# Two products with B sooner, turnings one scan step sooner, and 512 columns a matmul in ten products

## The chip, the cores and the metric

The kernel runs on one core of one Trainium2 chip. The metric is the device time of one launch in microseconds (us); the comparison is with the kernel before, on the same chip. Engines are called by the profile's names: PE (matmuls), PEld (its weight loads), DVE (vector), ACT (scalar), POOL and SP (which here mostly issue DMAs).

## The reference, cut to what is computed

All inputs are bf16; S = 2048 positions, D = 1024 channels, P = 1024 states.

```
x  = A_x
g  = sigmoid(sum(x * gate_w))                       # one gate per position
# branch A: a diagonal complex state space
Bu = x @ B_bar^T                                    # B_bar = (Lam_bar - 1)/Lam * (B_re + i B_im)
h[t] = Lam_bar * h[t-1] + Bu[t]                     # for t = 0..2047
a  = 2 * Re(h @ C^T) + x * Dskip
# branch B: a 4-tap filter, a product, a long convolution over 2048 positions
kv = shift_filter(k, shift_k) * v
b  = x * (conv(kv, ssm_k) + kv * ssm_D)
out = g * a + (1 - g) * b
```

## The kernel before

The first half (to about 212 us) does branch B: the long convolution as products with tables of cosines and sines, with its result `cv_scr` left in DRAM. The second half does most of branch A. The change lies almost wholly there.

**Tiling.** Positions come in `NTB` = 4 time blocks `tb` of 512, states in `NG` = 4 groups `g` of 256 (two tiles `j` of 128). In a time block the positions are split in odd and even ones, 256 each (`HB`): the scan runs over even positions only, with the squared factor, and odd ones follow from it. So there are 16 *scan steps* `j` = 0..15, one for each (`tb`, `g`), all on DVE.

**B products.** `Bu(i)` makes the input of one scan step; here `B8` is the product number 8. The list `order` says which (`tb`, `g`) a number stands for: the scan steps 4..15 use the numbers 2, 3, 8, 9, 4, 5, 10, 11, 12, 13, 14, 15. A product has two tiles, each made by `Bu_plain` (numbers 4, 5 and 8 to 15) or `Bu_tile` (the others). `Bu_plain` makes an *odd* and an *even* accumulator in PSUM, each with 16 matmuls of 256 columns, and ACT copies each to the tile U.

**Accumulators.** All products and rows draw their PSUM accumulators from one pool of four (`ps2`), in rotation: each one needs the accumulator drawn four before it to have been evicted by ACT.

**Turnings.** The products of `Bu_plain` have to be turned before their scan: `turn_U` (generators `turns_U[i]`) has ACT write lambda times the odd inputs to a buffer Q, one half of it at each of two calls, and then issues on POOL two DMAs (`gather`) that add Q to U, the second after the first has landed, as both add to the same place. There are two Q buffers: a turning waits for the second gather of the turning two before. (`turn_C`, which turns the matrices C, is another thing, and ended by step 4.)

**Rows.** `Cy_row(k)`, here `Ck`, is the product with C of 128 positions: 32 matmuls of 512 columns on PE into one accumulator, an eviction by ACT (`scale_a`, to `ga`), then `combine(k)`: a gather on POOL that adds the other branch, and on SP the write of the output; behind it on SP the loads of row k+3 (`loads`), and then on ACT `scale_b` of row k+2, which waits for that row's load (two ACTIVATEs, `pbb` and `gd`) and has a gather on POOL of its own. The last four rows are made together at the end of the kernel, from four accumulators (called F0 to F3 here), group after group of states.

**Order.** Engines run what is issued to them in order of program (`put` ties each engine's instructions to a chain). The string list `plan` gives, for each step j, the products and rows that follow the DVE work of that step; the first half of a turning is issued ahead of them (`step(turn)`), the second half and its gathers behind them (`run(turn)`).

Of the kernel before, what the change touches and what calls it, by code (L numbers as in the profile page):

```python
# [10 lines left out]
ACT = mybir.ActivationFunctionType  # L11
# [9 lines left out]
def kernel(  # L21
# [35 lines left out]
    ND = D // 128  # L57
# [3 lines left out]
    NTB = S // TB  # L61
    HB = TB // 2
# [23 lines left out]
    def ps2(shape, name):  # L86
        return psum.tile(shape, F32, name=name, tag="ps")
# [4 lines left out]
    def put(eng, f, *a, **kw):  # L92
        with tc.issue_after(prev[eng]) if eng in prev else nullcontext():
            i = f(*a, **kw)  # L94
        prev[eng] = getattr(i, "ins", i)

    def mm(o, l, r, first, last):
        put("pe", nc.tensor.matmul, o, lhsT=l, rhs=r, start=first, stop=last)
# [18 lines left out]
    def act(o, i, **kw):  # L117
        put("act", nc.scalar.activation, out=o, in_=i, **kw)
# [94 lines left out]
    BT = [bt_pool.tile([128, 2, ND, 256], BF16, name=f"BT{g}") for g in range(NG)]  # L213
# [5 lines left out]
    def load_xT(tb, halves=(0, 1), held=False):  # L219
        if 0 in halves:  # L220
            xTs[tb] = (xt_pool if tb in (1, 2) else xt_first).tile([128, ND, TB], BF16, name="xT", tag="xT")
        for h in halves:
            if held:
                hold(xTs[tb][:, 0, h * HB:h * HB + 1])
            load_t(xTs[tb][:, :, h * HB:(h + 1) * HB], xf[tb * TB + h:(tb + 1) * TB:2, :])
# [13 lines left out]
    def flat(ap):  # L239
        return ap.rearrange("p a b -> p (a b)")  # L240
# [412 lines left out]
    def gate(tb):  # L653
        psg = ps2([128, 2, 512], "p")[:, 0, 0:4]
        for tl in range(4):
            for dt_ in range(ND):
                mm(psg[:, tl:tl + 1], xTs[tb][:, dt_, tl * 128:(tl + 1) * 128], gwb[:, dt_:dt_ + 1],
                   dt_ == 0, dt_ == ND - 1)
        gates_of(slice(tb * 4, tb * 4 + 4), psg)
# [13 lines left out]
    ends = consts.tile([128, 2, NG, 2, 2], BF16, name="ends")  # L673
# [12 lines left out]
    def Bu(i):  # L686
        tb, g = order[i]
        if i in (10, 11):
            if i == 10:
                s5p["u2"] = xt_pool.tile([128, 2, 2 * (4 * HB + 4)], BF16, name="U2", tag="xT")  # L690
            U = s5p["u2"][:, i - 10]
        else:
            shape = [128, 2 * (4 * HB + 4)]
            if i in (6, 7, 8, 15):
                U = u4(shape, BF16, "U")
            else:
                home = uu[0 if i in (0, 1, 13, 14) else 1] if i < 6 or i in (13, 14) else s5p["uu"]
                U = home.tile(shape, BF16, name="U")
        if i in (4, 5) or i >= 8:
            V_, O_ = U[:, 0:4 * HB], U[:, 4 * HB:]  # L700
            V_ = V_.rearrange("p (c j t) -> p c j t", c=2, j=2)
            O_ = O_.rearrange("p (c j t) -> p c j t", c=2, j=2)
            Us[tb, g] = V_, O_[:, :, :, 2:]
            turns_U[i] = turn_U(g, V_, O_)
            return [Bu_plain(tb, g, V_, O_, j) for j in range(2)]
        U = U[:, 0:8 * HB].rearrange("p (a c j t) -> p a c j t", a=2, c=2, j=2)
        Us[tb, g] = U[:, 0], U[:, 1]
        return [Bu_tile(tb, g, U, j, (i, j) == (2, 1)) for j in range(2)]
# [25 lines left out]
    turns_U = {}  # L734

    def Bu_plain(tb, g, V_, O_, j):
        xT = xTs[tb]
        if j == 0:
            act(O_[:, :, :, 1], ends[:, 1 - tb % 2, g], func=ACT.Copy)
        for a, o in ((1, O_[:, :, j, 2:]), (0, V_[:, :, j])):  # L740
            ps = ps2([128, 2, HB], ("even", "odd")[a])
            for c in range(2):
                for dt_ in range(ND):
                    mm(ps[:, c], BT[g][:, c, dt_, j * 128:(j + 1) * 128], xT[:, dt_, a * HB:(a + 1) * HB],
                       dt_ == 0, dt_ == ND - 1)
            act(o, ps, func=ACT.Copy)
            if a == 1 and j == 1 and tb < NTB - 1:
                act(ends[:, tb % 2, g], O_[:, :, :, HB + 1], func=ACT.Copy)
        yield

    def turn_U(g, V_, O_):
# [73 lines left out]
    def loads(t_):  # L825
        if t_ < NT - 4:
            pbb = s5p["io"].tile([128, D], BF16, name="pbb", bufs=3)
            xr = s5p["io"].tile([128, D], BF16, name="xr", bufs=3)
        else:
            pbb, xr = bt_row(0, t_ - NT + 4), bt_row(1, t_ - NT + 4)  # L830
        move(pbb.rearrange("p (c d) -> p c d", d=128), cv_scr[:, :, t_ % 4, t_ // 4].rearrange("c p d -> p c d"))
        move(xr, rows_of(xf, t_))
        ios[t_] = pbb, xr

    def scale_b(t_):

        pbb = ios[t_][0]
        act(pbb, pbb, func=ACT.Identity, scale=omg[:, t_:t_ + 1])
        if t_ < NT - 4:
            gd = s5p["io"].tile([128, D], BF16, name="gd", bufs=1)  # L840
        else:
            gd = bt_row(3, t_ - NT + 4)
        act(gd, rows_, func=ACT.Identity, scale=gcols[:, t_:t_ + 1])
        gather(pbb, gd)
# [52 lines left out]
    def step(gen):  # L897
        next(gen, None)

    def run(gen):  # L900
        for _ in gen:
            pass
# [5 lines left out]
    none = iter(())  # L908
# [139 lines left out]
    c = NC - 1  # L1048
# [103 lines left out]


    NS = NTB * NG
    plan = ["B8", "B9 B10", "B11", "B12 C0", "C1", "C2", "C3", "B13", "C4 B14", "C5", "B15 C6", "C7", "C8", "C9", "C10", "C11"]
    rows = dict(scaled=0)

    def between(j):
# [5 lines left out]
    def prepare():  # L1164
        scale_b(rows["scaled"])
        rows["scaled"] += 1
# [3 lines left out]
    def advance(j):  # L1170
        step(scans[j])
        if j + 1 < NS:
            step(scans[j + 1])
        run(scans[j])
# [12 lines left out]
    for j in range(NS):  # L1187
        if 10 <= j < 14:
            loads(j + 2)
        advance(j)  # L1190
        for t in turning[2 * j:2 * j + 2]:
            run(t)
        on_act += [lambda t=t: step(t) for t in turning[2 * j + 2:2 * j + 4] for _ in range(2)]
        turn = turns_U[{3: 8, 4: 9, 5: 4, 6: 5}.get(j, j + 3)] if 2 < j < 13 else none
        step(turn)
        for unit in plan[j].split():
            (Bu_next if unit[0] == "B" else Cy_row)(int(unit[1:]))
        run(turn)
        if j < 3:
            prepare()  # L1200
        if 11 <= j < 15:
            scale_b(j + 1)
        if j == 0:
            load_xT(3)
            loads(2)
        if j == 8:
            gate(3)

    tb = NTB - 1
    t0 = tb * 4  # L1210
    pss = []
    for tl in range(4):
        ps = ps2([128, 2, 512], "psy")
# [42 lines left out]
```

## Time and profile before

| | |
|---|---|
| median of 3 runs | 414.16 us (413.93 to 414.62) |
| the profiled execution | 414.18 us |
| its span, first to last instruction | 412.4 us |
| busy: PE / DVE / ACT / POOL | 392.5 / 381.1 / 279.6 / 65.4 us |
| mean granted TensorE clock | 0.992 |
| PE, DVE, ACT busy in 300 to 320 us | 14.16 / 19.42 / 14.38 us, clock 0.83 |
| gathers of turnings (U<-Q) | 20, 256 KB each, 4.3 us to landing (median) |

The span is read from the instructions' records; the execution's own time is 1.8 us longer. Busy times are shares of one span and say by themselves nothing of what an engine waits for: the waits and the order of time do that. Nearly all instructions go through helper functions, so they have one line (L94), and groups are told apart by the names of the tiles, as in `psy<-CT,hb` (a row), `odd<-xT,BT` (a product with B) or `U<-Q` (a turning's gather).

### The profile page before, as it was taken

To read this page: it belongs to the slowest core of one execution; us is meant where nothing else is said; L and a number is where in the kernel's file an instruction comes from. 1 tells how busy PE (TensorE), PEld (TensorE's weight loads), DVE (VectorE), ACT (ScalarE), POOL (GpSimd) and SP (SyncE) were. 2 spreads that over 40 slices of the span, in tenths; PEclk is the share of its full clock that TensorE was granted. 3 is DMA by queue.
4 is the path that set the end of the run, shared out by engine and by line. 5 is a ranking of instruction groups with operands and counts; after the bars stand their busy time and mean duration, and the time that the engine had idled before them with its cause. 6 is when DMAs were issued, how large, how long until landed. Compare 5 with 4: busy or idle time off the path is not lost. (4 is left out here: it accounts for less than half of the span.)

```text
span 412.4 us, 7364 instructions
## 1 busy us (share of the span) xinstructions
PE 392.5 (95%) x2853; PEld 246.5 (60%) x2853; DVE 381.1 (92%) x618; ACT 279.6 (68%) x420; POOL 65.4 (16%) x88
## 2 busy tenths in 40 slices
PE   8999899999999999999989999999939999999895
PEld 5456366474755666576968888644716674444342
DVE  8799999999999999998999999999899997698954
ACT  4897986969698896565655699647585475675301
POOL 3011030302011020200000000022324123343300
PEclk9999999999999999999999999999979999999999
DMA  7879994979679391596977991149895777999902
GB/s 154 154 161 223 186 264 82 219 170 216 117 118 212 66 239 31 126 133 112 194 154 165 202 197 27 27 97 196 163 198 104 151 145 159 214 233 239 195 27 103
DMA packets 128453, 63.68 MB, mean 154 GB/s; under 512 B 106265, under 2 KB 113185, under 8 KB 128418
## 3 DMA queue, kind: packets, MB, share of 16 engines
q1 hardware_dynamic: 117664, 42.22, 47.5%
q0 software_dynamic: 10672, 20.98, 29.5%
q8 instruction: 22, 0.36, 0.4%
q14 instruction: 13, 0.11, 0.1%
q10 hardware_dynamic: 82, 0.02, 0.0%
HBM read 12.86 MB, written 8.39 MB: 52 GB/s over the span
## 5 line engine op out<-in xcount | busy, mean ns | idle before, releaser
L94 PEld LDWEIGHTS <-BT 128*128 128x128 bf16 x1024 | 99.7, 98 | 13.1 <-issue 0.2
L94 PE MATMUL psy<-CT,hb 128*128 128x512 bf16 x256 | 58.8, 389 | 7.3 <-DVE q L94 7.3
L94 PE MATMUL even<-xT,BT 128*128 128x256 bf16 x512 | 61.1, 273 | 0.0
L94 PE MATMUL odd<-xT,BT 128*128 128x256 bf16 x512 | 61.1, 273 | 0.0
L94 PE MATMUL psy<-CT,U 128*128 128x512 bf16 x256 | 56.5, 379 | 1.8 <-ACT BT L94 1.2
L94 PEld LDWEIGHTS <-hb 128*128 128x128 bf16 x256 | 25.4, 100 | 39.0 <-issue 10.4
L94 PEld LDWEIGHTS <-U 128*128 128x128 bf16 x256 | 25.0, 98 | 32.1 <-issue 2.4
L94 ACT ACTIVATE Vh<-psv 128x1024 bf16<-128x1024 f32 x32 | 31.0, 1033 | 11.5 <-PE psv L94 11.5
L94 DVE TENSOR_TENSOR_SCAN W<-rv,init,A 128x256 bf16<-128x256 f32 x48 | 32.2, 731 | 0.0
L94 PE MATMUL taps<-dg,kT 128*128 128x128 bf16 x512 | 31.1, 223 | 0.0
L94 PEld LDWEIGHTS <-SF 128*128 128x128 bf16 x192 | 18.8, 98 | 20.0 <-issue 0.8
L94 PEld LDWEIGHTS <-kT 128*128 128x128 bf16 x512 | 29.8, 100 | 1.0 <-issue 0.2
L94 PE MATMUL psk<-eok,SF 128*128 128x512 bf16 (+1 forms) x128 | 29.4, 352 | 0.0
L94 POOL DMA_DIRECT2D U<-Q x20 | 20.2, 1028 | 51.9 <-issue 25.3
L94 POOL DMA_DIRECT2D G<-wkh x8 | 9.7, 1218 | 115.6 <-DVE wkh L94 115.6
L94 PE MATMUL psz<-G,CI 128*128 128x512 bf16 x64 | 24.3, 380 | 3.6 <-DVE G L94 3.1
L94 ACT ACTIVATE Q<-U,lam 128x512 bf16<-128x512 bf16 (+1 forms) x40 | 22.2, 605 | 7.8 <-DMA U<-Q 7.8
L94 POOL DMA_DIRECT2D pbb<-gd x12 | 10.9, 910 | 100.0 <-ACT U L94 79.6
L94 ACT ACTIVATE U<-odd 128x512 bf16<-128x512 f32 x32 | 19.1, 597 | 11.3 <-PE odd L94 11.1
L94 ACT ACTIVATE pbb<-pbb,omg 128x1024 bf16<-128x1024 bf16 x12 | 13.7, 1143 | 17.0 <-DMA pbb<-cv_scr 17.0
L94 ACT ACTIVATE U<-even 128x512 bf16<-128x512 f32 x32 | 19.1, 597 | 8.8 <-PE even L94 8.6
L94 PE MATMUL psz<-G,SI 128*128 128x512 bf16 x64 | 24.3, 379 | 0.0
(170 smaller groups left out, 774.3 us busy)
## 6 DMA issues: line engine op xcount, KB each, us to landing
U<-Q POOLq DMA_DIRECT2D x20, 256.0 KB, 4.3
G<-wkh POOLq DMA_DIRECT2D x6, 768.0 KB, 8.0
cv_scr<-cv SPq DMA_DIRECT2D x16, 256.0 KB, 2.6
v<-in_B_v_dram SPq DMA_DIRECT2D x3, 1024.0 KB, 9.8
pbb<-cv_scr SPq DMA_DIRECT2D x12, 256.0 KB, 4.3
xr<-in_A_x_dram SPq DMA_DIRECT2D x12, 256.0 KB, 5.1
pbb<-gd POOLq DMA_DIRECT2D x12, 256.0 KB, 4.2
ga<-xr POOLq DMA_DIRECT2D x8, 256.0 KB, 3.9
```

The costliest lines, as they stand in the source:

```text
L94: i = f(*a, **kw)
```

## The change

Three edits, in one:

1. In `Bu_plain`, the odd and the even accumulator become one of twice the size, and the two matmuls of 256 columns with the same weights become one of 512. Both evictions follow when the whole is made. A tile draws one accumulator from the pool where it drew two. This touches the ten products 4, 5 and 8 to 15 (the "pairs" of odd and even).
2. In `plan`, B14 goes from behind C4 to behind B13 (step 7), right behind the row C3; B15 from ahead of C6 to behind C4 (step 8).
3. The turning of product 5 goes from step 6 to the end of step 5, where the turning of product 4 is too; the turnings of 10 to 15 go from steps 7 to 12 to steps 6 to 11.

```diff
@@ Bu_plain
-        for a, o in ((1, O_[:, :, j, 2:]), (0, V_[:, :, j])):
-            ps = ps2([128, 2, HB], ("even", "odd")[a])
-            for c in range(2):
-                for dt_ in range(ND):
-                    mm(ps[:, c], BT[g][:, c, dt_, j * 128:(j + 1) * 128], xT[:, dt_, a * HB:(a + 1) * HB],
-                       dt_ == 0, dt_ == ND - 1)
-            act(o, ps, func=ACT.Copy)
-            if a == 1 and j == 1 and tb < NTB - 1:
-                act(ends[:, tb % 2, g], O_[:, :, :, HB + 1], func=ACT.Copy)
+        ps = ps2([128, 2, 2, HB], "both")
+        for c in range(2):
+            for dt_ in range(ND):
+                mm(flat(ps[:, c]), BT[g][:, c, dt_, j * 128:(j + 1) * 128], xT[:, dt_], dt_ == 0, dt_ == ND - 1)
+        act(O_[:, :, j, 2:], ps[:, :, 1], func=ACT.Copy)
+        if j == 1 and tb < NTB - 1:
+            act(ends[:, tb % 2, g], O_[:, :, :, HB + 1], func=ACT.Copy)
+        act(V_[:, :, j], ps[:, :, 0], func=ACT.Copy)
...
-    plan = ["B8", "B9 B10", "B11", "B12 C0", "C1", "C2", "C3", "B13", "C4 B14", "C5", "B15 C6", "C7", "C8", "C9", "C10", "C11"]
+    plan = ["B8", "B9 B10", "B11", "B12 C0", "C1", "C2", "C3", "B13 B14", "C4 B15", "C5", "C6", "C7", "C8", "C9", "C10", "C11"]
+    turned = dict(zip(range(3, 12), (8, 9, 4, 10, 11, 12, 13, 14, 15)))
...
-        turn = turns_U[{3: 8, 4: 9, 5: 4, 6: 5}.get(j, j + 3)] if 2 < j < 13 else none
+        turn = turns_U[turned[j]] if j in turned else none
         step(turn)
         for unit in plan[j].split():
             (Bu_next if unit[0] == "B" else Cy_row)(int(unit[1:]))
         run(turn)
+        if j == 5:
+            run(turns_U[5])
```

## The prediction

> **What bounds the kernel now.** I read the busy times by slices first, then the chain that ended last, then the waits, and then the order of time of PE, ACT and POOL behind 255 us. The slices show one place where the clock was not full:
>
> ```profile
> PE   8999899999999999999989999999939999999895
> ...
> PEclk9999999999999999999999999999979999999999
> ```
>
> The 30th slice (299 to 309 us) has PE busy for three tenths, and is followed by no other of its kind. The chain says that the end is PE's:
>
> ```profile
> 383.35 2.05 ACT BT L94 x2
> 385.40 0.04 issue
> 385.44 22.62 PE psy L94 x104
> 408.06 0.03 issue
> ```
>
> ACT's evictions (`BT`, of C10 and C11) release F3, the last accumulator of the last four rows; from there PE runs without a gap to 408.06. DVE ended its scans at 395.27, while PE reached the last group of states, which needs them, at 400.98: DVE has 5.7 us to spare there. PE in order of time:
>
> ```profile
> 291.21 1.91 PE L94 MATMUL odd<-xT,BT 128*128 128x256 bf16 x16
> 292.95 1.91 PE L94 MATMUL even<-xT,BT 128*128 128x256 bf16 x16
> 294.70 1.91 PE L94 MATMUL odd<-xT,BT 128*128 128x256 bf16 x16
> 296.62 1.91 PE L94 MATMUL even<-xT,BT 128*128 128x256 bf16 x16
> 305.83 9.33 PE L94 MATMUL psy<-CT,hb 128*128 128x512 bf16 x32 [7.31 <-DVE q L94]
> ```
>
> B13 ends at 298.5, and C4 begins 7.3 us later. The profile names DVE, but C4's operands were ready. ACT shows who it was:
>
> ```profile
> 300.04 1.15 ACT L94 ACTIVATE pbb<-pbb,omg 128x1024 bf16<-128x1024 bf16 x1 [3.47 <-DMA pbb<-cv_scr]
> ...
> 304.95 0.20 ACT L94 ACTIVATE U<-ends 128x4 bf16<-128x4 bf16 x1
> 305.19 0.60 ACT L94 ACTIVATE U<-odd 128x512 bf16<-128x512 f32 x1
> ```
>
> C4 takes over the accumulator of B13's first odd half, whose eviction ended at 305.79. ACT came to it late: a row's load, then that row's scaling, then six ACTIVATEs of turnings. The clock fell to one half at 303.6 (granted mean 0.63 from 303.5 to 304.0), 5.1 us after the last matmul, and C4 took 9.33 us where a row takes 6.91 (64 matmuls in 13.82 us, 216 ns each). So this place costs 7.3 + 2.4 = 9.7 us of PE. POOL sets the pace of turnings:
>
> ```profile
> 291.67 1.83 POOL L94 DMA_DIRECT2D U<-Q  x1
> 298.40 0.86 POOL L94 DMA_DIRECT2D U<-Q  x1 [4.91 <-DMA U<-Q]
> ...
> 303.13 1.12 POOL L94 DMA_DIRECT2D U<-Q  x1
> 310.46 1.74 POOL L94 DMA_DIRECT2D U<-Q  x2 [6.21 <-issue]
> ```
>
> Between a turning's two gathers lie 4.85, 7.4, 6.7, 7.3, 4.8, 4.1, 6.4, 6.7, 5.4 and 6.2 us, 6.0 in the mean; what POOL has behind the first (row gathers) waits too. The second lands 3.4 to 5.5 us after its issue, 4.4 in the mean, read from DVE's waits for it.
>
> **512 columns.** 64 matmuls of 256 columns take 6.99 us a product (16 in 1.747); 32 of 512 take 6.91 by the rows' 216 ns. That is 0.08 a product, 0.8 for ten. Weight loads (98 ns, half as many) lie beside matmuls in either form. Products 4 and 5 end ahead of a wait of 1.18 us for DVE (`psz`, at 212.79) and gain nothing. B8 to B12 gain 0.4, and C0 0.15 more: it began at 263.58, right behind the eviction at 263.54 of B12's first odd half, four accumulators before it; now that is a tile of B11. So C0 to C3, their loads and the turnings behind them come 0.55 us sooner. The evictions read half of a larger tile, which no row shows; the bounds are the 0.58 and 0.62 us of the 64 evictions there are, and I take no change. They start up to 1.75 us later for the odd half, with nobody waiting. If 512 columns cost what twice 256 do, 0.8 us in all is lost from the sum.
>
> The Trainium skill ("TensorE: Matmul & The Clock Gate", Back-to-back issue gap) gives some 131 ns for a sustained matmul of 512 columns. By that the three products on the path would gain 8 us; the rows' 216 ns speak against it, and I give it no chance.
>
> **Step 5 and 6, the price of two turnings in one step** (all times with the 0.55 us off). Turning 5 needs turning 9's Q, as before: ACT does both its halves by 296.4, where it did one. Then comes the first half of turning 10, which needs turning 4's Q: its second gather goes at 297.9 and lands 4.4 later, at 302.3. (The scan of product 4 began at 303.27 without a wait, so it landed by then.) ACT stands still until then, with C3's eviction behind it: 302.3 + 1.4 (half a turning) + 1.1 = 304.8, against 296.57 before. On PE, B13 ends at 297.55, B14's first tile at 301.0, and its second tile needs C3's accumulator: it runs from 304.8 to 308.25, after 3.8 us of idling. ACT goes on with a row's scaling (2.1) and half of turning 10 (1.4), to 308.2; then the first half of turning 11 needs turning 5's Q: gathers at 298.5 and 304.5, landing 308.9. So 308.9 + 1.4, and 1.3 for B13's first evictions (as at 304.95 to 306.27): C4 starts at 311.6, after another 3.35 us of idling. Both gaps are under 5.1 us, so I take the clock to stay.
>
> **PE from there.** C4 to 318.5 (before 315.0), B15 to 325.4, the gate 0.8, C5 to 333.1 (329.7), C6 to 340.0 (343.6), and C11, if nothing stops PE, to 374.5 (378.1): 3.6 us sooner. That is 9.7 less the new gaps of 7.15, with 0.55 from C0, 0.24 from three products, and 0.2 from the small wait at 296.45.
>
> **The end.** F3 needs C11's eviction. Before, its chain ran from row 8's gather (POOL, 365.31): write of the output (371.93), load of row 11 (ACT at 377.04), scaling of rows 11 and 14, eviction of C10, scaling of row 15, eviction of C11, F3 at 385.44: 20.1 us. In the new order row 8's gather stands behind turning 15's (one step sooner) and row 12's. C5 is evicted at 334.25; its gather, output (5.0) and the load behind (0.4 + 4.4) let row 8 be scaled at 344.1; C6's gather goes at 343.5 behind turning 13's second, so row 9's load lands at 353.3; its scaling (2.1) and 0.6 of turning 15 put that turning's gathers at 356.0 and 362.0, row 12's at 362.6, row 8's at 363.2. Add 20.1: F3 at 383.3, 2.1 us sooner. So of PE's 3.6 us, ACT's chain lets 2.1 through.
>
> The moved turnings also take away DVE's waits for them (7.7 us in six, all but one of 1.07); row 7's product meets a new wait of some 3.5 us, its `pbb` landing at 340.7. DVE ends near 392, with PE at the last group near 399: neither sets the end.
>
> **Sum.** 414.18 (the profiled execution; the median is 0.02 lower) less 2.1: 412.1 us.
>
> **Rivals.** (a) *Short latencies*: with gathers 4.3 us apart, as in the two shortest rows, ACT and not POOL sets C4 (310.9), and the chain at the end comes in under PE, which then ends at 374.55 - 0.7 + 27.6 = 401.5 against 408.06: 407.6, or 408.3 with C4 as forecast. For it: fewer transfers run beside turning 5's gathers than before. Against: six of ten pairs lay 6.2 us or more apart.
>
> (b) *Slower: turning 5 holds ACT until the clock falls.* The place is the gap between B14 and C4. If turning 5's gathers take the long ends, 7.4 and 5.5, they land at 311.4, C4 starts at 314.1, after 5.85 us, and takes 9.3: it ends at 323.4, not 318.5. All behind it moves by 4.9: 417.0. It decides from 5.1 us of idling, a landing at 310.7. For it: the gap at this very place did so before. Against: it asks for long values twice.
>
> (c) *The same: the clock falls in the gaps as forecast.* Of B14's second tile it would cost nothing (ACT lets C4 go later anyway); of C4, 2.4 us: 414.5. The trace shows no fall after its gaps of 1.2 us, and one 5.1 us into a longer one; what 3.8 does it doesn't show. The skill's same page (What's actually happening) has the clock halved after an idle window of about 3.4 us that runs free of the program; by it gaps of 3.35 and 3.8 would seldom hold a whole window, and the 5.1 us of the trace agree.
>
> (d) *The same: the loop of rows gives all back.* If row 8's gather goes at 365.3 as before (its predecessors each some 0.7 us longer), F3 stays at 385.4: 414.2.
>
> **Chances.** Forecast 0.38 (own range 410.8 to 413.3), (a) 0.17, (b) 0.30, (c) and (d) 0.15. A measurement of this kernel can tell some 0.2%, 0.83 us, from no change. Faster is the forecast and (a), 0.55; same 0.15; slower 0.30. The range goes from (a) with C4 as forecast, less half a us, to (b)'s price: 407.8 to 417.0.
>
> **What would show it.** Right: no matmul `odd` or `even` of B8 to B15, 32 of 512 columns in 6.91 us; two idle spells of PE between 300 and 312 us in place of one, both under 5 us, clock full; C3's eviction near 305, C4 near 311.6, C6's end near 340, F3 near 383 released by ACT; DVE's waits for U<-Q down to about 1 us. Wrong: C4 later than 313.4 or over 9 us long (b); F3 without a wait for ACT (a); a DVE wait late enough that the last group waits for its scan, which would have my order of engines wrong.

## The result, and the profile after

The changed kernel takes 417.25 us (median of 5 runs, 416.79 to 417.80); the kernel before, in runs on the same chip, 413.93. The ratio is 1.0086, 95% interval 1.0064 to 1.0109: 0.9% slower, where 0.5% faster was forecast. The profiled execution took 417.25 us, its span is 415.5 us, 3.1 more than the 412.4 of before.

PE and its clock in 40 slices, after (10.4 us a slice):

```profile
PE   8999899999999999999989999999959999994995
...
PEclk9999999999999999999999999999969999998799
```

There are two falls of the clock now: the old place (30th slice) and a new one, the 37th and 38th slice, 374 to 395 us. The chain that ended last:

```profile
382.71 2.05 ACT BT L94 x2
384.75 0.04 issue
384.80 26.38 PE psy L94 x112
411.18 0.03 issue
```

The end still goes from ACT's evictions by way of the last accumulators to PE, as before; but the accumulator that PE stood for is C10's now, taken over by F2 (112 matmuls follow where 104 did), and the whole lies 3.1 us later (411.2 against 408.06). PE in order of time:

```profile
290.72 10.52 PE L94 MATMUL both<-xT,BT 128*128 128x512 bf16 x48
305.82 5.88 PE L94 MATMUL both<-xT,BT 128*128 128x512 bf16 x16 [4.58 <-ACT ga L94]
311.95 7.07 PE L94 MATMUL psy<-CT,hb 128*128 128x512 bf16 x32 [0.25 <-ACT U L94]
...
374.90 3.62 PE L94 MATMUL psy<-CT,hb 128*128 128x512 bf16 x16
384.80 5.64 PE L94 MATMUL psy<-CT,U 128*128 128x512 bf16 x16 [6.28 <-ACT BT L94]
390.28 3.62 PE L94 MATMUL psy<-CT,hb 128*128 128x512 bf16 x16
```

C11 ended at 374.9, 3.2 us sooner than the 378.14 of before. Then F0 and F1 (16 matmuls), 6.28 us of waiting for C10's accumulator, and F2 and F3 at a low clock: 5.48 us to the next line where 16 matmuls take 3.45. What held C10 and C11, on ACT and SP:

```profile
379.48 1.15 ACT L94 ACTIVATE pbb<-pbb,omg 128x1024 bf16<-128x1024 bf16 x1 [7.64 <-DMA pbb<-cv_scr]
...
383.66 1.09 ACT L94 ACTIVATE BT<-psy,gcols 128x1024 bf16<-128x1024 f32 x1
...
386.73 1.09 ACT L94 ACTIVATE BT<-psy,gcols 128x1024 bf16<-128x1024 f32 x1
```

```profile
373.25 0.34 SPq L94 DMA_DIRECT2D out_dram<-BT  x1
373.68 0.41 SPq L94 DMA_DIRECT2D pbb<-cv_scr  x1
```

POOL, with the two gathers of turning 13, C6's gather behind them, and row 8's gather:

```profile
337.76 1.12 POOL L94 DMA_DIRECT2D U<-Q  x1
344.89 0.86 POOL L94 DMA_DIRECT2D U<-Q  x1 [6.00 <-DMA U<-Q]
345.47 1.16 POOL L94 DMA_DIRECT2D ga<-xr  x1
...
365.85 1.55 POOL L94 DMA_DIRECT2D BT<-xr  x1
```

Row 11's load is issued at 373.68 behind the write of row 8, which waited for row 8's gather (POOL, 365.85); ACT could scale row 11 only at 379.48 (before 377.04), and the evictions of C10 (383.66) and C11 (386.73) stand behind that on ACT. At the first place, ACT stands ahead of C3's eviction:

```profile
303.25 1.12 ACT L94 ACTIVATE Q<-U,lam 128x512 bf16<-128x512 bf16 x2 [6.14 <-DMA U<-Q]
304.28 0.49 ACT L94 ACTIVATE Q<-U,mlam 128x256 bf16<-128x256 bf16 x1
304.68 1.09 ACT L94 ACTIVATE ga<-psy,gcols 128x1024 bf16<-128x1024 f32 x1
```

That is the first half of turning 10, waiting for a Q buffer. In the profiled spans the 3.1 us come out so: C5, which has one product more ahead of it now (B15), is evicted 3.8 us later (333.67 against 329.90); from there to C11's eviction it took 1.3 less (53.1 against 54.4), so F3's accumulator came 2.4 later; and the slow clock in F2 and F3 cost 0.7 beyond that. The evictions of C5 and C11 on ACT, before and after:

```profile
329.90 1.11 ACT L94 ACTIVATE ga<-psy,gcols 128x1024 bf16<-128x1024 f32 x1 [4.18 <-PE psy L94]
...
384.29 1.10 ACT L94 ACTIVATE BT<-psy,gcols 128x1024 bf16<-128x1024 f32 x1
```

```profile
333.67 1.11 ACT L94 ACTIVATE ga<-psy,gcols 128x1024 bf16<-128x1024 f32 x1 [3.64 <-PE psy L94]
...
386.73 1.09 ACT L94 ACTIVATE BT<-psy,gcols 128x1024 bf16<-128x1024 f32 x1
```

And the waits of F2 and F3 on PE before, 0.6 and 1.2 us:

```profile
382.36 1.89 PE L94 MATMUL psy<-CT,U 128*128 128x512 bf16 x8 [0.60 <-DVE q L94]
385.44 1.89 PE L94 MATMUL psy<-CT,U 128*128 128x512 bf16 x8 [1.19 <-ACT BT L94]
```

### The profile page after: what moved, and what is told of

The parts are those of the page before. It is cut to its first block, busy times and chain, and to the rows that moved or that the text cites. A ratio compares the mean times of both kernels' runs of the same rounds, so it can differ in the third digit from the quotient of the medians.

```text
span 415.5 us, 6731 instructions
## 1 busy us (share of the span) xinstructions
PE 393.3 (95%) x2533; PEld 215.7 (52%) x2533; DVE 381.2 (92%) x618; ACT 278.5 (67%) x420; POOL 65.3 (16%) x88
## 5 line engine op out<-in xcount | busy, mean ns | idle before, releaser
L94 PEld LDWEIGHTS <-BT 128*128 128x128 bf16 x704 | 69.0, 99 | 48.4 <-issue 7.9
L94 PE MATMUL both<-xT,BT 128*128 128x512 bf16 x320 | 72.5, 387 | 4.6 <-ACT ga L94 4.6
L94 PE MATMUL psy<-CT,U 128*128 128x512 bf16 x256 | 58.4, 388 | 6.3 <-ACT BT L94 6.3
L94 PE MATMUL psy<-CT,hb 128*128 128x512 bf16 x256 | 56.6, 379 | 0.2 <-ACT U L94 0.2
L94 ACT ACTIVATE U<-both 128x512 bf16<-128x512 f32 x40 | 21.9, 595 | 12.1 <-PE both L94 11.9
L94 ACT ACTIVATE Q<-U,lam 128x512 bf16<-128x512 bf16 (+1 forms) x40 | 22.3, 606 | 10.1 <-DMA U<-Q 10.1
L94 DVE TENSOR_TENSOR U<-U,q 128x512 bf16<-128x512 bf16 (+2 forms) x51 | 23.5, 488 | 0.6
L94 PE MATMUL even<-xT,BT 128*128 128x256 bf16 x192 | 22.9, 273 | 0.0
```

## The experiments

**Which edit does what.** Each edit alone, and the first two. The reasons in the texts on record are called theory 1: a *loop of rows* sets the end (eviction of row k, its gather on POOL, its write on SP, the load of row k+3 behind that, its scaling on ACT, and the next eviction behind that).

`e_cols`, edit 1 alone (the `Bu_plain` of the diff, nothing else):

> The kernel before with edit 1 alone (512 columns, one accumulator a tile). C4 then takes over C2's accumulator, free since 285.6, so PE should go through B13 into C4 at 298 and end it near 306.4 (scan 7 is ready at 304.6) in place of 315.0. Theory 1 (the loop of rows sets the end: eviction, gather, write of the output, load of row k+3, scaling, at some 10 us a row from C6 on): PE is up to 8 us early, but ACT's evictions from C6 on move by 0 to 4 us only, PE stands still for 3 us or more ahead of F2 or F3, and the time is 410 to 414. Rival (PE's own work sets the end): 406 to 408, no wait at F2 or F3.

Measured 410.06 us, ratio 0.990 (0.987 to 0.993). C4 no longer waits for ACT (it ran from 297.87, with 1.47 us for scan 7), C5 is evicted at 324.99, C11 at 380.0, 4.3 us sooner than before; F2 and F3 waited only 1.3 and 1.2 us. The time sits at theory 1's lower edge, and the wait of over 3 us that it named wasn't there; the rival's 406 to 408 didn't come either.

`e_turn`, edit 3 alone:

```diff
+    turned = dict(zip(range(3, 12), (8, 9, 4, 10, 11, 12, 13, 14, 15)))
...
-        turn = turns_U[{3: 8, 4: 9, 5: 4, 6: 5}.get(j, j + 3)] if 2 < j < 13 else none
+        turn = turns_U[turned[j]] if j in turned else none
...
+        if j == 5:
+            run(turns_U[5])
```

> The kernel before with edit 3 alone (turning 5 in step 5 too, 10 to 15 one step sooner). Theory 1 (the doubled turning in step 5 puts rows 3 to 5 back, and the loop of rows carries that to the end): C3's eviction near 305 and C4 near 311.6 as in the changed kernel, with nothing to fill the gap; row 11's load lands 2 to 4 us later than the 377.0 of before; 417 to 419. Rival (only DVE's waits matter): DVE loses its 7.7 us of waits for gathers, and the time falls to 410 to 413.

Measured 420.9, ratio 1.0168 (1.0141 to 1.0194): 7 us slower. PE stood 8.5 us for C3's eviction (303.57) within B13, with nothing to do. The rival is out.

`e_cols_plan`, edits 1 and 2 without 3:

> Edits 1 and 2 without edit 3 (turnings at the steps of before). C3 is evicted near 296.5, B14 runs on to 304.8, C4 starts near 306.3. Theory 1 (loop of rows): C6 ends near 335, 8 us sooner than before, yet C10 and C11 are evicted near 382 and 385 as before, PE waits 6 us or more for F2 with a fall of the clock, and the time is 413 to 416. Rival (the doubled and earlier turnings alone cost the 3 us, and PE sets the end): 405 to 409.

Measured 413.2, ratio 0.9978 (0.9955 to 1.0002; the runs spread from 409.8 to 414.8). Much as theory 1 said: C11 ended on PE at 371.7, 6.4 us ahead of before, and PE then waited 5.65 us for F2 with a fall of the clock; C11's eviction came 1.4 us sooner only.

`e_plan`, edit 2 alone:

> The kernel before with edit 2 alone (B14 behind B13, B15 behind C4, matmuls of 256 columns and two accumulators a tile). B14's first half needs the accumulator of B13's first half, evicted at 305.8, so B14 fills the gap no sooner than C4 did and C4 comes 7 to 9 us later than the 305.8 of before. Theory 1 (loop of rows): rows 4 and 5 are put back by 7 us, the end by 4 to 7: 418 to 421. Rival (order of products is worth nothing either way, since PE is late only at the end): 413 to 415.

Measured 419.36, ratio 1.0132 (1.0093 to 1.0172), as theory 1 said: PE stood 6.9 us for B13's accumulators ahead of B14, and C5's eviction moved to 337.4. Without edit 1's spare accumulators the new place of B14 can't fill the gap.

So edit 1 gains some 4 us, edit 2 behind it gives back 3, and edit 3 costs 4 more.

**Is it the loop of rows?** Two edits on the changed kernel. `f_tail` gives PE other work while C10 and C11 are not evicted:

```diff
-    for g in range(NG - 1):
-        for tl in range(4):
-            Cy_g(tb, tl, pss[tl][0], g, False)
+    for half in ((0, 1), (2, 3)):
+        for g in range(NG - 1):
+            for tl in half:
+                Cy_g(tb, tl, pss[tl][0], g, False)
```

> The changed kernel with one more edit: of the last four rows, F0 and F1 go through the first three groups of states before F2 and F3 do. PE then has 10.4 us of work at hand (6 x 8 matmuls of 216 ns) when it stands before F2's accumulator now. Theory 1 (the loop of rows evicts C10 and C11 late, and the 6.3 us wait plus the cold clock behind it is what that costs): no wait for F2 or F3, the clock stays full, PE ends near 402.5 in place of 411.2, and the time is 408 to 410. Rival (something else sets the end, as DVE's last scan or the transfers): less than 3 us gained, 414 or more.

Measured 409.58, ratio 0.9889 (0.9869 to 0.9910), against 1.0086 for the changed kernel without it. PE of `f_tail`:

```profile
375.22 10.52 PE L94 MATMUL psy<-CT,hb 128*128 128x512 bf16 x48
385.58 1.89 PE L94 MATMUL psy<-CT,U 128*128 128x512 bf16 x8
387.86 8.79 PE L94 MATMUL psy<-CT,U 128*128 128x512 bf16 x40 [0.39 <-ACT BT L94]
```

C11 was evicted no sooner (386.71), but PE waits 0.4 us in place of 6.3, at full clock. So the loss at the end was this wait, and no other engine stood right behind it.

`f_load` takes the write out of the loop (shown is the place of the calls; `loads` is also split in two, `load_pbb` and `load_xr`):

```diff
     def Cy_row(k):
         Cy(k // NG, k % NG)
+        if k + 3 < NT - 4:
+            load_pbb(k + 3)
         combine(k)
         if k + 3 < NT - 4:
-            loads(k + 3)
+            load_xr(k + 3)
```

> The changed kernel with one more edit: the load of row k+3's pbb is issued on SP ahead of row k's output, so it no longer stands behind a write that waits for a gather. Theory 1a (the loop is a chain of latencies through SP): ACT's waits for pbb<-cv_scr fall from 24.0 to under 8 us, row 11 is scaled 4 us or more sooner than at 379.5, and the time falls to 408 to 412. Theory 1b (the loop goes at the rate of the DMA engines, which are over 100% busy from 340 to 380 us): the waits only change places, row 11 is scaled at 377 or later, 415 to 418.

Measured 409.39, ratio 0.9878 (0.9856 to 0.9900). ACT's waits for `pbb` loads, from 255 us on, of the changed kernel and then of `f_load`:

```profile
ACT pbb L94 <- DMA pbb<-cv_scr: 24.0, 6, 7.6
```

```profile
ACT pbb L94 <- DMA pbb<-cv_scr: 2.6, 2, 2.2
```

Row 11 is scaled at 367.56, 11.9 us sooner. Theory 1a holds, and 1b (the rate of the DMA engines) is out: their busy share stayed at 1.04 to 1.08 from 340 to 380 us, and the order of issue alone made the difference. Some of ACT's waiting did change places: its waits for a Q buffer grew from 10.1 to 15.0 us, and 6.1 us for the gather `pbb<-gd` are new.

The same on the kernel before, `f_load_before`:

> The kernel before with the pbb loads ahead of the outputs on SP, alone. Theory 1a (the same loop of rows also sets the end of the kernel before, whose F2 and F3 wait 0.6 and 1.2 us for ACT): ACT's waits for pbb<-cv_scr fall from 17.0 to under 5 us and C5 to C11 are evicted sooner, but PE is the bound right behind: 1.5 to 4 us faster, 410 to 412.5. Rival (in the kernel before, PE alone sets the end): 413 to 414.5, unchanged.

Measured 409.28, ratio 0.9902 (0.9885 to 0.9920): the loop bound the kernel before too, by more than expected. In the profile some 3 of the 5 us come at C4, where ACT no longer waits 3.5 us for a row's load ahead of B13's evictions (C4 ends at 311.88, before at 315.00), and the rest at F2 and F3, whose waits of 0.6 and 1.2 us are gone.

`g_c5`, edit 1 with B14 moved the other way (`"C4", "C5 B14"` in place of `"C4 B14", "C5"`):

> Edit 1 alone, and B14 moved the other way: from behind C4 to behind C5, so that only B13 stands ahead of C5. Theory 1 (the end follows C5's eviction by some 46 us to row 11's scaling and 54 to C11's eviction, whatever PE does): C5 is evicted near 320 to 322 in place of 325.0, and the time is 406 to 409. Rival (the place of the products is worth nothing once the accumulators are saved): 409.5 to 411, as edit 1 alone.

Measured 409.04, ratio 0.9887 (0.9863 to 0.9912), between the two forecasts. C5 was evicted at 321.27 as forecast, but C6 stood behind two products then, and the way from C5 to C11 took 57.3 us, not 54. Its gain over edit 1 alone is within the intervals. So C5's eviction is not the one start of the loop; the spacing of the rows counts too.

**What of edit 3 costs.** `e_double` puts the turnings 10 to 15 back, and keeps the doubled step 5:

```diff
-    turned = dict(zip(range(3, 12), (8, 9, 4, 10, 11, 12, 13, 14, 15)))
+    turned = {3: 8, 4: 9, 5: 4, 7: 10, 8: 11, 9: 12, 10: 13, 11: 14, 12: 15}
```

> The changed kernel with half of edit 3 undone: turning 5 stays doubled in step 5, but the turnings 10 to 15 are back at steps 7 to 12. Theory 1 (what edit 3 costs is the doubled step, which puts C3's eviction to 305, C4 to 312 and so C5's eviction to 333; from there the loop takes some 46 us to row 11's scaling): 416 to 418 as the changed kernel. Rival (what it costs is that turnings 10 to 15 take the DMA engines from row loads a step sooner): 412.5 to 414, as with edits 1 and 2 alone.

Measured 409.93, ratio 0.9898 (0.9876 to 0.9921). My theory fell: the doubled step by itself costs nothing, it even helps (413.2 without it; C4 began 1.1 us sooner, and at full clock). The rival's 412.5 to 414 was not met either. C3 was evicted at 297.25 and C5 at 328.05. What had put C3 back was not turning 5 but the first half of turning 10, issued in step 6 ahead of C3's eviction while no Q buffer was free. `h_behind` tests that: the changed kernel, with those first halves behind:

```diff
-        step(turn)
+        if j not in (6, 7):
+            step(turn)
```

> The changed kernel with one line more: in the steps 6 and 7 the first half of the turning (10 and 11) is issued behind the step's row or products, not ahead. The doubled step 5 and all turnings one step sooner stay. Theory 2 (what edit 3 costs is ACT standing for a Q buffer, 6.1 us, ahead of C3's eviction, and again ahead of B13's): C3 is evicted near 297.3 in place of 304.7, PE doesn't wait for B14's second tile, C4 starts at 307 to 308, and the time is 409 to 413. Rival (the earlier turnings cost by their transfers and their place on POOL ahead of the rows): C3 sooner, but row 11 is scaled at 378 or later, 415 to 418.

Measured 414.34, ratio 1.0015 (0.9998 to 1.0031), between the two forecasts. C3 (296.79) and C4 (307.26) came as theory 2 said, which recovers 2.9 of the 7.8 us between the changed kernel and `e_double` (0.0071 and 0.0188 of 414). The rest was still open, so the late and the early turnings were parted. `i_early` (`6: 10, 7: 11, 9: 12, 10: 13, 11: 14, 12: 15`, with the line of `h_behind`):

> Turnings 10 and 11 in steps 6 and 7 (whole turnings behind the step's units), 12 to 15 back at steps 9 to 12, step 8 without one. Theory 3 (the remaining cost lies with the late turnings): 409 to 411, as with all of 10 to 15 put back. Rival (it lies with the early ones, by ACT's order in steps 6 to 8): 413 to 415.

Measured 413.86, ratio 0.9993 (0.9970 to 1.0015): the rival's range. ACT's work for turning 10 lies ahead of B13's evictions in step 7, so C4 started 1.1 us later than in `e_double`, at a low clock, and C5 was evicted 2.8 later. `i_late` (`7: 10, 8: 11, 9: 13, 10: 14, 11: 15`, and turning 12 at the end of step 8):

> Turnings 10 and 11 back at steps 7 and 8, 12 at the end of step 8 too, 13 to 15 in steps 9 to 11 as in the changed kernel. Theory 3 (late turnings, one step sooner, stand ahead of the rows on POOL and the DMA engines): C5 is evicted near 328, but rows 8 to 11 come late, row 11 is scaled at 374 or later, 413 to 416. Rival (early ones): 409 to 411.

Measured 417.82, ratio 1.0084 (1.0060 to 1.0108), worse than either forecast. Its doubled step, 8, is followed by a first half ahead of C5's eviction. ACT of `i_late`:

```profile
331.50 1.12 ACT L94 ACTIVATE Q<-U,lam 128x512 bf16<-128x512 bf16 x2 [5.83 <-DMA U<-Q]
332.53 0.49 ACT L94 ACTIVATE Q<-U,mlam 128x256 bf16<-128x256 bf16 x1
332.93 1.09 ACT L94 ACTIVATE ga<-psy,gcols 128x1024 bf16<-128x1024 f32 x1
```

C5 had ended on PE at 327.6 and was evicted at 332.93: the Q wait of the changed kernel, at another place. So this run can't say by its time what the late turnings alone cost. A third Q buffer, which would bear on the wait itself, was not tried.

Put together, in us of the profiles:

| kernel | C5 evicted | row 11 scaled | C11 evicted | C5 to C11 |
|---|---|---|---|---|
| before | 329.9 | 377.0 | 384.3 | 54.4 |
| edits 1 and 2 (`e_cols_plan`) | 330.5 | 375.7 | 382.9 | 52.4 |
| turnings 10 to 15 put back (`e_double`) | 328.1 | 371.6 | 378.8 | 50.8 |
| early ones sooner (`i_early`) | 330.8 | 374.2 | 381.5 | 50.6 |
| all sooner, behind the units (`h_behind`) | 329.0 | 374.8 | 382.1 | 53.1 |
| after | 333.7 | 379.5 | 386.7 | 53.1 |
| late ones sooner (`i_late`) | 332.9 | 380.0 | 387.3 | 54.3 |

(In the first row B15 lies between C5 and C6, in the others it does not.) Early turnings act on C5's eviction; the rows with turnings 13 to 15 one step sooner take 53 to 54 us from there, the others, leaving the first row aside, 51 to 52. These are single executions; runs of `e_cols_plan`, `h_behind` and `i_early` spread by 3 to 5 us, and the profiled ones of the last two were 1.6 and 2.1 us faster than their medians. That the late turnings cost some 2 us in the loop is read from three rows against three (and from `e_turn` against before, both with B15 between: 56 against 54.4), not shown by an experiment that changes nothing else.

**A version that beats both.** `h_double_tail_load` is `e_double` with the edits of `f_tail` and `f_load`:

> A version to beat both: the changed kernel with the turnings 10 to 15 back at steps 7 to 12, the last rows two by two, and the pbb loads ahead of the outputs on SP. Theory 1a (once rows are no longer held by the loop, PE's own work sets the end): C11 ends on PE near 372.7, no wait for F2 or F3, PE ends near 397 to 400: 403 to 407. Rival (DVE's last scan, 391 to 396 so far, becomes the bound, or the transfers): 407 to 409.

Measured 401.44 us, ratio 0.9709 (0.9694 to 0.9723): 2.9% faster than before, and below the 403 to 407 of theory 1a. PE runs without a wait from 290.75 to the end (a few matmul records are missing from this trace, so that 47 stand for 48):

```profile
367.53 10.52 PE L94 MATMUL psy<-CT,hb 128*128 128x512 bf16 x47
377.89 10.52 PE L94 MATMUL psy<-CT,U 128*128 128x512 bf16 x47
388.25 3.62 PE L94 MATMUL psy<-CT,hb 128*128 128x512 bf16 x16
```

`h_behind_tail_load`, the same two edits on `h_behind`:

> The changed kernel with the first halves of the turnings 10 and 11 behind their step's units, the last rows two by two, and the pbb loads ahead of the outputs. Theory 2 with 1a: C4 starts near 307 to 308, PE runs on without a wait from there, and ends near 398 to 400: 404 to 407, as near to the other version as a few tenths of a per cent. Rival (sooner turnings take transfers from the rows even then): slower than the other version by 2 us or more.

Measured 402.14, ratio 0.9730 (0.9713 to 0.9748), below its forecast too, and 0.2% above the other version; the rival's 2 us or more weren't there. `f_cols_tail_load`, on edit 1 alone:

> Edit 1 alone, with the last rows two by two and the pbb loads ahead of the outputs. Theory 1a (with the loop mended, PE's own work sets the end, and only PE's idle time ahead of C4 and C5 is left for edit 2 to fill): PE waits some 1.5 us for scan 7 and up to 2.3 ahead of C5, ends 2 to 4 us later than in the best version so far: 403 to 405.5. Rival (edits 2 and 3 are worth nothing by then): 401 to 402.5.

Measured 402.55, ratio 0.9727 (0.9710 to 0.9743): at the rival's upper edge, not theory 1a's 403 to 405.5. With the loop mended and other work for PE at the end, the order of turnings and products is worth some 0.2%, and the intervals of the three overlap; without the mending, the place of the turnings alone was worth nearly 2% (1.0086 against 0.9898). So what the place of the turnings costs goes mostly by way of the loop and the wait at the end. The changed kernel itself, with those first halves ahead, was not run with both edits; with one of them it takes 409.4 to 409.6.

## Why the prediction was wrong, by its steps

- **512 columns: right.** 48 matmuls from 290.72 end near 301.1, as forecast; C0 began at 263.09 against 263.58 before. Edit 1's real worth, though, is the accumulators: alone it gains some 4 us, where I gave 0.8 to its matmuls, and saw only C0 among what the spare accumulators free.
- **Steps 5 and 6: right.** B14's second tile began at 305.82 (forecast 304.8), C4 at 311.95 (311.6). The reason in the text's heading, two turnings in one step, was wrong in part: `e_double` has them and no loss. The wait for Q that I described there in the same lines is the cause. C4's time is met in part by luck: turning 4's Q came 1 us later than forecast (303.25, not 302.3), but ACT then didn't stand for turning 5's Q, whose gathers lay at most 5.3 us apart, not 6.0.
- **The clock: wrong, without a price there.** "Both gaps are under 5.1 us, so I take the clock to stay." It fell at 303.6, 2.4 us after the last matmul. The rival (c) had this right: of B14's second tile it cost nothing.
- **PE from there: right.** C6 ended at 340.4 (340.0), C11 at 374.9 (374.5). Row 7's product waited 3.1 us on DVE (3.5).
- **The end: wrong, and this decided.** C5's eviction ended at 334.8 (334.25). Row 8's gather went at 365.85, not 363.2: the two gathers of turning 13 lay 7.1 us apart, not 6.0, so C6's gather behind them went at 345.47, not 343.5, and the load of row 9 landed 2.6 us later than I had it. From row 8's gather to row 11's scaling it took 13.6 us, not 11.7: the write went 0.8 us later behind the gather, and the load took 5.8 us from issue to scaling, not 4.7. So from C5's eviction to C11's I summed 49.0 us and it took 53.0. The same stretch in the profile of before is 54.4 us; I had built the sum from single latencies and never held it against that row. It alone gives the sign: C5 3.8 us later, and a loop that takes as long as before or 1.3 less. F3's accumulator was free at 387.8, not 383.3; these 4.5 us are most of the 5.2 between forecast and result. Rival (d) had the gather almost right (365.3), but not what follows it.
- **What PE's lead is worth: wrong.** My sum went by F3's accumulator alone, and gave neither a wait nor a price to C10's, which F2 takes over; by its own figures PE would have stood some 2 us there (0.6 + 3.6 - 2.1). PE was 3.2 us early and the accumulator 2.4 late, so a wait of 0.6 became 6.3, long enough for the clock to fall, which cost 0.7 us beyond the late accumulators. That (b)'s price of 417.0 lies next to the measured 417.25 is chance: its gap ahead of C4 wasn't there, and C4 took 7.1 us.

As the Trainium skill ("TensorE: Matmul & The Clock Gate", What's actually happening) has it, the clock follows windows of 3413 ns that run free of the program. The trace agrees with the windows: the falls of the changed kernel, at 303.6 and 382.1, lie 23.0 of them apart, and each slow spell lasted two. It does not agree that a window must be idle as a whole: PE was busy for the first 1.0 us of the one that ended at 303.6.

```profile
303.60:303.80 0.20, 0.00 (x0) 0.00 (x0) 0.20 (x1) 0.20 (x1) 0.00 (x0) 0.52 1.24 215
...
382.00:382.20 0.20, 0.00 (x0) 0.00 (x0) 0.20 (x2) 0.20 (x1) 0.20 (x1) 0.79 0.00 0
```

(Busy time of each engine in stretches of the changed kernel; the third column from the end is the granted clock, 0.50 when low.)

## What to carry to other kernels

Where work goes round a loop over several engines and queues, a sum of single latencies is to be held against the same loop's length in the profile of before; here that one subtraction gives the sign. (The stretch from C5 to C11 took 50.6 to 57.3 us in the kernels that kept the order of loads, so it is a check on a sum and no constant.) An engine that gets ahead of such a loop gains nothing and can lose its clock while it waits: give it other work for that time, or shorten the loop by taking out of each queue what stands ahead of the next turn without need (here a load behind a write that waits for a transfer). And an instruction that waits for a buffer is issued behind the evictions that others wait for, not ahead of them.

## What was not expected of the hardware

The clock fell 2.4 us after the last matmul, and gaps of 2.7 us (`e_cols_plan`, C4 8.4 us long in place of 7.1) and 3.05 us (`i_early`, 8.8) cost too, while one of 2.65 us (`h_behind`) didn't: the place of the gap in the windows counts, not its length alone. The traces bear this out: within one trace, changes of the granted clock lie whole multiples of 3.413 us apart, to 0.02 us. Counted so, the gap of `e_cols_plan` has 2.1 us in the window that ended with the fall at 306.78; that of `h_behind`, counted back from its fall at 377.67, is parted by an edge at 305.99 into 1.4 and 1.3 us. Between 250 and 400 us of the traces in which such an edge can be placed, each window at full clock in which PE idled for 2.1 us or more was followed by a fall, and none with 1.8 us or less was, but for one of `e_cols` (1.6 us idle, fall at 315.87) that also held 0.9 us of the gate's one-column matmuls. No run was made to test that.

DMA engines at a busy share of 1.07 to 1.11 for 40 us looked like a limit and were none: with the loads issued in another order (`f_load`), at a share of 1.04 to 1.08, row 11 was scaled 12 us sooner.
